# A causal-attention mixer on one core: the second halves of the first batch's probabilities go through TensorE, and the planner is told when to load w_ch1

## The chip, the cores and the metric

The kernel runs on one core of one Trainium2 chip. The metric is device time in microseconds (us); lower is better. A core has five engines that run side by side, each with its own in-order queue: TensorE (PE, whose weight loads the profile lists as PEld), VectorE (DVE), ScalarE (ACT), GpSimd (POOL) and SyncE (SP, whose queue here issues every DMA).

## The reference, cut to what matters

Three stages run one after the other on two batches of 448 tokens, twelve heads of width 64, 768 channels:

```python
scores = scale * q @ k.T                      # causal mask, per head: 448 x 448
attn = exp(scores - max) / sum                # 24 (batch, head) pairs
x = attn @ v                                  # -> (2, 448, 768)
u = x + (relu(x.T @ w_tok1) @ w_tok2).T       # token mixing, 448 -> 256 -> 448
y = u + relu(u @ w_ch1) @ w_ch2               # channel mixing, 768 -> 1536 -> 768
h = gelu(y @ w_in); a, b = split(h)           # 768 -> 1024
out = y + (a * (w_sg @ norm(b) + b_sg)) @ w_out
```

The weights arrive in 64-bit floats. Each operand of a product is split into a high and a low part, and a product is three matmuls (high x high, high x low, low x high).

## The kernel before

**Attention.** A head's 448 queries are four tiles (one of 64 rows, three of 128). They are worked in two halves of 512 key columns each: half 0 holds tiles 0 and 3, half 1 holds tiles 1 and 2 (`HALVES`). There are 2 batches x 12 heads x 2 halves = 48 halves; a step n of the main loop (`order`) is one head, so two halves. `pair` runs two heads that share a tile of PSUM for the values.

`probabilities` makes one half: TensorE computes the scores into PSUM (line 284); VectorE negates, scales, masks and reduces them to the negated maximum `mx` in one pass (L289), then adds the logarithm of PSCALE = 32768 to the two maxima in a small instruction of 128x2 (L294, `bias`); ScalarE takes the exponential (L296), so that `pe` holds probabilities times 32768; ScalarE casts them to 16 bits (L298, the high half of `hl`); GpSimd subtracts that from `pe` (L299, the low half); and one DMA on SP's queue transposes both halves at once into `pT` (L301). `values` (L324 to L326) multiplies `pT` by the values on TensorE.

**Values.** `prep_v` splits the values of a pair of heads into 16-bit parts with a scale (L253 to L261), and uses one PSUM slot of the pool `ps_e` (two slots) for a small matmul.

**Token mixing.** After every fourth head `token_mix` runs for that group: `a_ps`, then `u_ps` (L375, L377), which also adds x by fp32 transposes on TensorE (L384), then the split into `u_hi` and `u_lo` (L386, L387). The token weights are loaded at step n = 3 (`load_tok`).

**Channel mixing.** `channel_up(m, batches)` loads one tile of w_ch1 (`load64`: a DMA at L105 on SP into one of two `wraw` slots, ScalarE at L112, VectorE at L113 to L115, ScalarE at L119, GpSimd at L94), then does 18 matmuls (`r_ps`, L134 to L136) per batch. For m from 0 to 6 (`NF0` = 7) batch 0 is done in the attention part, with a PSUM slot of `ps_e`; in program order the first stands after step (1, 6) and the other six behind the loop. Everything after (`channel_up` for batch 1, `channel_down`, the gated part) is a dense run of matmuls.

**Order of the work.** The order on each engine is not the program's: a planner simulates a timeline when the kernel is built, and takes what is ready by priority, where program order is the priority (`prep_v` is moved ahead by 80). So a channel_up that stands late in the program is a filler: it goes where the planner's timeline has room. What the planner has laid down is then fixed on each in-order queue.

Of the kernel before, what the change touches and what calls it, by code (L numbers as in the profile page):

```python
# [10 lines left out]
F16 = mybir.dt.float16  # L11
F32 = mybir.dt.float32
F32R = mybir.dt.float32r
I32 = mybir.dt.int32
AF = mybir.ActivationFunctionType
ALU = mybir.AluOpType
# [3 lines left out]
PSCALE = 32768.0  # L20
# [7 lines left out]
def mixer_kernel(  # L28
# [18 lines left out]
    nc = tc.nc  # L47
    B, H2, D2, S = q.shape
    H, D = 2 * H2, D2 // 2
# [3 lines left out]
    P = 128  # L53
# [10 lines left out]
    def f32(ap):  # L64
        return ap.bitcast(F32)
# [5 lines left out]
    ident = const.tile([P, P], F32, name="ident")  # L71
# [21 lines left out]
    def sub(lo, src, hi):  # L93
        nc.gpsimd.tensor_sub(lo, src, f32(hi))  # L94
# [27 lines left out]
    def load_w(src):  # L122

        k = src.shape[1]
        hi = wpool.tile([P, WC // P, P], F32R, tag="whi", name="whi", bufs=3)[:, :k, :]
        lo = wpool.tile([P, WC // P, P], F32R, tag="wlo", name="wlo", bufs=3)[:, :k, :]
        load64(hi.rearrange("p a f -> p (a f)"), lo.rearrange("p a f -> p (a f)"), src.rearrange("p a f -> p (a f)"))
        return hi, lo

    def mm3(ps, pairs, begun=False):  # L130

        n = len(pairs)
        for i, ((lh, ll), (rh, rl)) in enumerate(pairs):
            nc.tensor.matmul(ps, lh, rh, start=i == 0 and not begun, stop=False)  # L134
            nc.tensor.matmul(ps, lh, rl, start=False, stop=False)  # L135
            nc.tensor.matmul(ps, ll, rh, start=False, stop=i == n - 1)  # L136
# [19 lines left out]
    NP = 512  # L156
# [8 lines left out]
    rpool = rs.enter_context(tc.tile_pool(name="rpool", bufs=1))  # L165
    r_of = {}

    def channel_up(m, batches, pool, psum):

        wh, wl = load_w(w_ch1[m])  # L170
        for b in batches:
            us = slice(b * S, (b + 1) * S)
            pr = psum.tile([P, 512], F32, tag="d", name="r_ps")
            mm3(pr[:, :S], [((wh[:, c, :], wl[:, c, :]), (u_hi[:, c, us], u_lo[:, c, us])) for c in range(NCC)])
            rh = pool.tile([P, S], F32R, tag=f"rh{m}_{b}", name="rh")
            rl = pool.tile([P, S], F32R, tag=f"rl{m}_{b}", name="rl")
            nc.scalar.activation(rh, pr[:, :S], AF.Relu)
            nc.vector.scalar_tensor_tensor(rl, pr[:, :S], 0.0, f32(rh), ALU.max, ALU.subtract)
            r_of[m, b] = (rh, rl)
# [14 lines left out]
    with ExitStack() as at:  # L194
# [3 lines left out]
        hlp = at.enter_context(tc.tile_pool(name="hlp", bufs=2))  # L198
        stp = at.enter_context(tc.tile_pool(name="stp", bufs=6))
# [5 lines left out]
        ps_e = at.enter_context(tc.tile_pool(name="ps_e", bufs=2, space=PSUM))  # L205
# [18 lines left out]
        for i in range(NVT):  # L224
            hi = fixed.tile([P, NVC, 2, D + 2], F16, name=f"vh{i}")
# [5 lines left out]
        def load_tok():  # L231
            for c in range(NQ):
                load64(w1h[:, c, :], w1l[:, c, :], w_tok1[tok(c), :], "pool", twice=c == 0)
            for c in range(NT):
                load64(w2h[:, c, :], w2l[:, c, :], w_tok2[c * P:(c + 1) * P, :], "pool")
# [27 lines left out]

        count = [0]

        def probabilities(qp, k2, hd, half):

            ps = ps_s.tile([P, NP], F32, tag="s", name="s_ps")  # L270
            if (hd, half) == (1, 0):
                pe, mx = pes[count[0] % len(pes)], mxs[count[0] % len(pes)]
            else:
                pe = xp.tile([P, NP], F32, tag="pe", name="pe", bufs=NPE)
                mx = stp.tile([P, 2], F32, tag="mx", name="mx")
            todo, o = [], 0
            for j, i in enumerate(HALVES[half]):
                w = KW[i]
                if i > 0 or hd == 0:
                    todo.append((j, i, slice(o, o + w)))  # L280
                    q0 = S - 64 if i == 0 else S + w - P if hd else w - P - 64
                    for ks in KEYS[i]:
                        m = ks.stop - ks.start
                        nc.tensor.matmul(ps[:, o:o + m], qp[:, q0:q0 + P], k2[:, ks], start=True, stop=True)  # L284
                        o += m
                else:
                    o += w
            for j, i, cs in todo:
                nc.vector.tensor_tensor_reduce(  # L289
                    out=pe[:, cs], in0=ps[:, cs], in1=mask0 if i == 0 else mask[:, MASKS[i]],  # L290
                    scale=-1.0 / math.sqrt(D), scalar=3.0e38, op0=ALU.add, op1=ALU.min, accum_out=mx[:, j:j + 1],
                )
            bias = stp.tile([P, 2], F32, tag="bias", name="bias")
            nc.vector.tensor_scalar(bias, mx, math.log(PSCALE), None, ALU.add)  # L294
            for j, i, cs in todo:
                nc.scalar.activation(pe[:, cs], pe[:, cs], AF.Exp, bias=bias[:, j:j + 1], scale=-1.0)  # L296
            hl = hlp.tile([P, 2, NP], F16, tag="hl", name="hl", bufs=4)
            nc.scalar.copy(hl[:, 0], pe)  # L298
            nc.gpsimd.tensor_sub(hl[:, 1], pe, hl[:, 0])  # L299
            pT = hlp.tile([P, 2, NP // P, P], F16, tag="pT", name="pT", bufs=4)  # L300
            nc.sync.dma_start_transpose(  # L301
                out=pT.rearrange("p a c q -> p (a c) q"), in_=hl.rearrange("p a n -> p (a n)")
            )
            return pT


# [21 lines left out]
        def pair(b, e, qk, vs, x):  # L328

            (vh, vl, sv), (xf, xh, xl) = vs, x  # L330
            px = ps_x.tile([P, 7, D + 1], F32, tag="x", name="x_ps")
            for hd in range(2):
                for half in range(2):
                    pT = probabilities(*qk, hd, half)
                    values(px, pT, hd, half, vh, vl)
                if hd == 0:
                    yield
            count[0] += 1
            rd = stp.tile([P, 7, 1], F32, tag="rd", name="rd")
            nc.vector.tensor_scalar(rd, px[:, :, D:D + 1], 1e-9 * PSCALE, sv[:, 0:1], ALU.add, ALU.mult)  # L340
            nc.vector.reciprocal(rd, rd)
            nc.vector.tensor_mul(xf[:, e], px[:, :, :D], rd.to_broadcast([P, 7, D]))
            cs = slice(e * P, (e + 1) * P)
            x6 = xf[:, e, 1:].rearrange("p (c h) d -> p c (h d)", h=2)
            nc.scalar.copy(xh[:, 1:, cs], x6)
            sub(xl[:, :, cs], x6, xh[:, 1:, cs])

            for h in range(2):
                hs, ls = (slice(64 * i, 64 * i + 64) for i in (h, 1 - h))
                ds = slice(e * P + h * D, e * P + h * D + D)  # L350
                nc.gpsimd.tensor_scalar(xh[hs, 0, ds], xf[hs, e, 0], 1.0, 0.0, ALU.mult, ALU.add)
                sub(xh[ls, 0, ds], xf[hs, e, 0], xh[hs, 0, ds])

        def token_mix(b, g, xf, xh, xl):
# [13 lines left out]
            for e in range(N // P):  # L368
# [17 lines left out]
                nc.scalar.copy(u_hi[:, cc, us], pu[:, :S])  # L386
                nc.vector.tensor_sub(u_lo[:, cc, us], pu[:, :S], f32(u_hi[:, cc, us]))  # L387

        order = [(b, h) for b in range(B) for h in range(H)]
        qks, vss = {}, {}  # L390

        def prepare(n):
            if n < len(order):
                b, h = order[n]
                if h % 2 == 0:
                    qks[b, h // 2] = prep_qk(b, h // 2)

        def prepare_v(n):
            if n < len(order) and n % 2 == 0:
                b, h = order[n]  # L400

                with tc.high_priority(offset=-80):
                    vss[b, h // 2] = prep_v(b, h // 2)

        dense = list(range(NF0))
        for n in range(AHEAD):
            prepare(n)
        for n in range(VAHEAD):
            prepare_v(n)
        for n, (b, h) in enumerate(order):  # L410
            prepare(n + AHEAD)
            prepare_v(n + VAHEAD)
            if n == GH - 1:
                load_tok()
            if h % GH == 0:
                x = (
                    xp.tile([P, GH // 2, 7, D], F32, tag="xf", name="xf", bufs=2),
                    xp.tile([P, NQ, GH * D], F32R, tag="xh", name="xh"),
                    xp.tile([P, NQ - 1, GH * D], F32R, tag="xl", name="xl"),
                )  # L420
            if h % 2 == 0:
                it = pair(b, h % GH // 2, qks[b, h // 2], vss[b, h // 2], x)
            next(it, None)
            if h % GH == GH - 1:
                token_mix(b, h // GH, *x)

            if (b, h) == (1, H // 2):
                channel_up(dense.pop(0), [0], rpool, ps_e)

        for m in dense:  # L430
            channel_up(m, [0], rpool, ps_e)


    NDC = 4
# [172 lines left out]
```

## Time and profile before

| | |
|---|---|
| time, median of 3 runs | 440.64 us (436.31, 440.64, 441.17) |
| the profiled execution's own time | 436.57 us |
| its span, first to last instruction | 434.8 us |
| PE busy | 403.1 us, 93% |
| DVE busy | 322.8 us, 74% |
| POOL busy | 251.4 us, 58% |
| ACT busy | 196.9 us, 45% |
| mean granted TensorE clock | 0.984 of full |

Busy times are unions over the whole span; TensorE's matmuls overlap one another and their ends are modelled, so a busy PE is not PE at its peak. The attention part fills about the first 165 us; the rest of the span is the dense run.

### The profile page before, as it was taken

To read this page: it belongs to the slowest core of one execution; us is meant where nothing else is said; L and a number is where in the kernel's file an instruction comes from. 1 tells how busy PE (TensorE), PEld (TensorE's weight loads), DVE (VectorE), ACT (ScalarE), POOL (GpSimd) and SP (SyncE) were. 2 spreads that over 40 slices of the span, in tenths; PEclk is the share of its full clock that TensorE was granted. 3 is DMA by queue.
4 is the path that set the end of the run, shared out by engine and by line. 5 is a ranking of instruction groups with operands and counts; after the bars stand their busy time and mean duration, and the time that the engine had idled before them with its cause. 6 is when DMAs were issued, how large, how long until landed. Compare 5 with 4: busy or idle time off the path is not lost. (4 is left out here: it accounts for less than half of the span.)

```text
span 434.8 us, 7061 instructions
## 1 busy us (share of the span) xinstructions
PE 403.1 (93%) x2567; PEld 340.1 (78%) x2567; DVE 322.8 (74%) x623; ACT 196.9 (45%) x341; POOL 251.4 (58%) x234
## 2 busy tenths in 40 slices
PE   5786897879879999999999999999999999999996
PEld 3363676667758899899999999999898889965995
DVE  5999996769999669889878677877786744159422
ACT  2777677575957544435344333333334133322200
POOL 2678877935996945456242355545539574225572
PEclk9999999969999999999999999999999999999999
DMA  7899999999798943534564533443434200200122
GB/s 206 179 211 235 221 182 216 196 247 239 181 190 218 168 147 95 197 145 146 148 190 131 157 100 121 123 144 121 154 133 139 93 0 6 92 2 1 64 107 84
DMA packets 66739, 62.30 MB, mean 143 GB/s; under 512 B 53136, under 2 KB 58384, under 8 KB 66704
## 3 DMA queue, kind: packets, MB, share of 16 engines
q1 hardware_dynamic: 66704, 61.85, 54.5%
q8 instruction: 20, 0.33, 0.3%
q14 instruction: 15, 0.12, 0.1%
HBM read 46.50 MB, written 2.75 MB: 113 GB/s over the span
## 5 line engine op out<-in xcount | busy, mean ns | idle before, releaser
L94 POOL TENSOR_TENSOR wlo<-wm,whi 128x768 fp32r<-128x768 f32 (+1 forms) x41 | 83.3, 2033 | 59.3 <-ACT whi L119 54.1
L112 ACT ACTIVATE wm<-wraw 128x768 f32<-128x768 f32 (+2 forms) x53 | 42.7, 808 | 79.1 <-DMA wraw<-in 39.6
L299 POOL TENSOR_TENSOR hl<-pe,hl 128x512 f16<-128x512 f32 x48 | 60.9, 1279 | 29.1 <-ACT hl L298 25.3
L284 PE MATMUL s_ps<-k,q 128*128 128x64 f32 (+3 forms) x216 | 58.9, 414 | 16.9 <-DVE mx L289 9.9
L113 DVE TENSOR_SCALAR wm<-wm 128x768 int32<-128x768 int32 (+2 forms) x53 | 34.2, 647 | 51.5 <-ACT wm L112 51.3
L114 DVE SCALAR_TENSOR_TENSOR wm<-wraw,wm 128x768 int32<-128x768 int32 (+2 forms) x53 | 64.7, 1221 | 0.8
L115 DVE SCALAR_TENSOR_TENSOR wm<-wraw,wm 128x768 int32<-128x768 int32 (+2 forms) x53 | 64.6, 1221 | 0.8
L296 ACT ACTIVATE pe<-pe,bias 128x192 f32<-128x192 f32 (+3 forms) x84 | 39.6, 523 | 33.0 <-DVE bias L294 32.6
L284 PEld LDWEIGHTS s_ps<-k,q 128*128 128x128 f32 x216 | 31.9, 207 | 28.9 <-DVE mx L289 11.5
L135 PE MATMUL r_ps<-u_lo,whi 128*128 128x448 f32 x144 | 53.4, 371 | 0.5 <-DVE u_lo L387 0.4
L134 PE MATMUL r_ps<-u_hi,whi 128*128 128x448 f32 x144 | 53.2, 370 | 0.0
L136 PE MATMUL y_ps<-rh,wlo 128*128 128x448 f32 x144 | 52.7, 366 | 0.3 <-POOL wlo L94 0.3
L136 PE MATMUL r_ps<-u_hi,wlo 128*128 128x448 f32 x144 | 52.7, 366 | 0.0
L134 PE MATMUL y_ps<-rh,whi 128*128 128x448 f32 x144 | 52.6, 366 | 0.0
L135 PE MATMUL y_ps<-rl,whi 128*128 128x448 f32 x144 | 52.6, 366 | 0.0
L119 ACT CAST whi<-wm 128x768 fp32r<-128x768 f32 (+1 forms) x41 | 32.7, 798 | 28.2 <-PE ug_ps L135 11.1
L289 DVE CUSTOM_DVE_ANT_0 pe<-s_ps,mask 128x192 f32<-128x192 f32 (+3 forms) x84 | 34.6, 439 | 4.4 <-PE s_ps L284 4.4
L94 POOL TENSOR_TENSOR u_lo<-yt,u_hi 128x448 fp32r<-128x448 f32 x12 | 15.3, 1273 | 35.5 <-ACT u_hi L191 35.5
L298 ACT CAST hl<-pe 128x512 f16<-128x512 f32 x48 | 28.6, 611 | 7.8 <-DMA pT<-hl 7.7
L324 PE MATMUL x_ps<-vh,pT 128*128 128x65 f16 (+1 forms) x240 | 26.3, 198 | 6.3 <-DMA pT<-hl 6.2
L324 PEld LDWEIGHTS <-pT 128*128 128x128 f16 (+1 forms) x240 | 21.4, 99 | 13.4 <-DMA pT<-hl 7.2
L135 PEld LDWEIGHTS r_ps<-u_lo,whi 128*128 128x128 f32 x144 | 27.2, 189 | 3.5 <-DVE u_lo L387 1.3
(141 smaller groups left out, 949.9 us busy)
## 6 DMA issues: line engine op xcount, KB each, us to landing
wraw<-in SPq DMA_DIRECT2D x35, 768.0 KB, 4.4
wraw<-in SPq DMA_DIRECT2D x14, 512.0 KB, 3.8
vr<-in SPq DMA_DIRECT2D x12, 320.0 KB, 3.5
k<-in SPq DMA_DIRECT2D x12, 224.0 KB, 3.4
q<-in SPq DMA_DIRECT2D x24, 112.0 KB, 3.6
out<-ob SPq DMA_DIRECT2D x12, 224.0 KB, 1.9
wraw<-in SPq DMA_DIRECT2D x3, 256.0 KB, 3.3
pT<-hl SPq DMA_TRANSPOSE x48, 3.5
```

Source lines behind the costliest of these rows:

```text
L94: nc.gpsimd.tensor_sub(lo, src, f32(hi))
L112: nc.scalar.activation(m, words.bitcast(F32)[:, :, 1], AF.Abs, scale=2.0 ** -112)
L114: nc.vector.scalar_tensor_tensor(mi, words[:, :, 1], -0x80000000, mi, ALU.bitwise_and, ALU.bitwise_or)
L115: nc.vector.scalar_tensor_tensor(mi, words[:, :, 0], 29, mi, ALU.logical_shift_right, ALU.bitwise_or)
L134: nc.tensor.matmul(ps, lh, rh, start=i == 0 and not begun, stop=False)
L135: nc.tensor.matmul(ps, lh, rl, start=False, stop=False)
L136: nc.tensor.matmul(ps, ll, rh, start=False, stop=i == n - 1)
L284: nc.tensor.matmul(ps[:, o:o + m], qp[:, q0:q0 + P], k2[:, ks], start=True, stop=True)
L289: nc.vector.tensor_tensor_reduce(out=pe[:, cs], in0=ps[:, cs], in1=mask0 if i == 0 else mask[:, MASKS[i]], scale=-1.0 / math.sqrt(D), scal ...
L296: nc.scalar.activation(pe[:, cs], pe[:, cs], AF.Exp, bias=bias[:, j:j + 1], scale=-1.0)
L299: nc.gpsimd.tensor_sub(hl[:, 1], pe, hl[:, 0])
L324: nc.tensor.matmul(o, ph, vh[:, c, h, :D + 1], start=j == 0, stop=False)
```

## The change

For batch 0 and half 1 (two per pair of heads, six pairs: 12 of the 48 halves) the probabilities are no longer cast, subtracted and transposed by DMA. The exponential takes `mx` itself as its bias, so `pe` is at most 1; TensorE transposes it in four fp32 pieces of 128x128 into a PSUM slot of `ps_e`; ScalarE writes the high half from PSUM with the factor 32768; VectorE writes the low half from PSUM in one pass. For the other 36 halves the sum with log(PSCALE) is taken by ScalarE (`nc.scalar.add`) and not by VectorE. The main loop records after each step the last DMA transpose that was issued, and every `channel_up` of the attention part puts its SP instructions (its w_ch1 load) behind the transpose of step 10 + m; the first of them moves in program order from behind step (1, 6) to behind step (1, 10).

```diff
-        def probabilities(qp, k2, hd, half):
+        def probabilities(qp, k2, hd, half, on_pe):
...
-            bias = stp.tile([P, 2], F32, tag="bias", name="bias")
-            nc.vector.tensor_scalar(bias, mx, math.log(PSCALE), None, ALU.add)
+            bias = mx
+            if not on_pe:
+                bias = stp.tile([P, 2], F32, tag="bias", name="bias")
+                nc.scalar.add(bias, mx, math.log(PSCALE))
             for j, i, cs in todo:
                 nc.scalar.activation(pe[:, cs], pe[:, cs], AF.Exp, bias=bias[:, j:j + 1], scale=-1.0)
+            pT = hlp.tile([P, 2, NP // P, P], F16, tag="pT", name="pT", bufs=4)
+            if on_pe:
+                tp = ps_e.tile([P, 512], F32, tag="d", name="t_ps")
+                for c in range(NP // P):
+                    cs = slice(c * P, (c + 1) * P)
+                    nc.tensor.matmul(tp[:, cs], pe[:, cs], ident, is_transpose=True, start=True, stop=True)
+                hi, lo = (pT[:, i].rearrange("p c q -> p (c q)") for i in range(2))
+                nc.scalar.activation(hi, tp, AF.Copy, scale=PSCALE)
+                nc.vector.scalar_tensor_tensor(lo, tp, PSCALE, hi, ALU.mult, ALU.subtract)
+                return pT
             hl = hlp.tile([P, 2, NP], F16, tag="hl", name="hl", bufs=4)
             nc.scalar.copy(hl[:, 0], pe)
             nc.gpsimd.tensor_sub(hl[:, 1], pe, hl[:, 0])
-            pT = hlp.tile([P, 2, NP // P, P], F16, tag="pT", name="pT", bufs=4)
-            nc.sync.dma_start_transpose(
+            last[0] = nc.sync.dma_start_transpose(
                 out=pT.rearrange("p a c q -> p (a c) q"), in_=hl.rearrange("p a n -> p (a n)")
-            )
+            ).ins
             return pT
...
-                    pT = probabilities(*qk, hd, half)
+                    pT = probabilities(*qk, hd, half, b == 0 and half == 1)
...
+        last, marks = [None], []
         order = [(b, h) for b in range(B) for h in range(H)]
...
         dense = list(range(NF0))
+
+        def up():
+
+            m = dense.pop(0)
+            with tc.issue_after(marks[H - 2 + m]):
+                channel_up(m, [0], rpool, ps_e)
...
             next(it, None)
+            marks.append(last[0])
             if h % GH == GH - 1:
                 token_mix(b, h // GH, *x)
 
-            if (b, h) == (1, H // 2):
-                channel_up(dense.pop(0), [0], rpool, ps_e)
-
-        for m in dense:
-            channel_up(m, [0], rpool, ps_e)
+            if (b, h) == (1, H - 2):
+                up()
+
+        while dense:
+            up()
```

## Rows read from the trace of the kernel before

**Rows 1.** Busy time per engine by stretch: us busy (instructions), clock, DMA share, GB/s.
```profile
...
0.00:87.00 87.00, 68.06 (x652) 47.77 (x652) 74.81 (x253) 56.25 (x113) 62.81 (x85) 0.98 0.94 206
87.00:165.00 78.00, 69.69 (x616) 59.02 (x616) 65.79 (x143) 49.41 (x89) 55.25 (x58) 0.93 0.84 194
165.00:435.00 270.00, 265.32 (x1302) 233.27 (x1300) 182.25 (x228) 91.24 (x140) 133.37 (x93) 1.00 0.34 108
...
```

**Rows 2.** The same, 10 to 60 us and stretches after it.
```profile
...
10.00:60.00 50.00, 40.26 (x379) 26.39 (x379) 49.08 (x152) 35.28 (x72) 38.02 (x42) 0.97 0.95 207
60.00:87.00 27.00, 22.98 (x264) 18.25 (x262) 20.82 (x79) 18.33 (x38) 22.69 (x30) 1.00 1.00 204
90.00:100.00 10.00, 10.00 (x82) 7.94 (x80) 8.35 (x17) 7.99 (x16) 4.97 (x4) 0.76 1.08 227
...
```

**Rows 3.** Waits, 0 to 87 us: us in total, times, longest.
```profile
...
ACT pe L296 <- DVE bias L294: 18.5, 10, 6.6
...
PEld s_ps L284 <- DVE mx L289: 8.9, 9, 2.0
PE s_ps L284 <- DVE mx L289: 7.8, 13, 1.3
...
```

**Rows 4.** Groups of instructions, VectorE, 10 to 60 us: busy us, mean ns.
```profile
...
L294 DVE TENSOR_SCALAR bias<-mx 128x2 f32<-128x2 f32 x22 | 9.5, 435 | 0.0
L261 DVE SCALAR_TENSOR_TENSOR vl<-vr,sv,vh 128x640 f16<-128x640 f32 x5 | 7.7, 1546 | 0.6 <-ACT vh L260 0.6
...
```

**Rows 5.** Timeline of VectorE, L294 twice: start us, us.
```profile
...
12.55 0.15 DVE L294 TENSOR_SCALAR bias<-mx 128x2 f32<-128x2 f32 x1
...
56.33 0.86 DVE L294 TENSOR_SCALAR bias<-mx 128x2 f32<-128x2 f32 x1
...
```

**Rows 6.** Groups by shape, 0 to 250 us: busy us, mean ns, idle before.
```profile
...
L299 POOL TENSOR_TENSOR hl<-pe,hl 128x512 f16<-128x512 f32 x48 | 60.9, 1279 | 29.1 <-ACT hl L298 25.3 <-DMA pT<-hl 3.1 <-DVE bias L294 0.3
...
L298 ACT CAST hl<-pe 128x512 f16<-128x512 f32 x48 | 28.6, 611 | 7.8 <-DMA pT<-hl 7.7
...
L294 DVE TENSOR_SCALAR bias<-mx 128x2 f32<-128x2 f32 x48 | 18.8, 402 | 0.1
...
L296 ACT ACTIVATE pe<-pe,bias 128x448 f32<-128x448 f32 x24 | 15.8, 658 | 2.7 <-DVE bias L294 2.7
...
L296 ACT ACTIVATE pe<-pe,bias 128x64 f32<-128x64 f32 x12 | 4.1, 346 | 19.5 <-DVE bias L294 19.5
L365 DVE SCALAR_TENSOR_TENSOR al<-a_ps,ah 128x512 fp32r<-128x512 f32 x6 | 4.1, 680 | 0.9 <-ACT ah L364 0.9
...
L364 ACT ACTIVATE ah<-a_ps 128x512 fp32r<-128x512 f32 x6 | 3.5, 589 | 0.4 <-PE a_ps L136 0.4
...
```

**Rows 7.** DMA queue totals (packets, MB, share) and transposes issued, 0 to 87 us.
```profile
...
q1 hardware_dynamic: 34663, 17.80, 93.6%
...
pT<-hl SPq DMA_TRANSPOSE x29, 3.6
...
```

**Rows 8.** DMA queue totals, 190 to 300 us.
```profile
...
q1 hardware_dynamic: 3164, 15.71, 46.3%
...
```

**Rows 9.** What touches pT, whole span: ns min/median/max, first and last start.
```profile
...
L301 SPq DMA_TRANSPOSE pT<-hl x48: 1232/1264/5275, 11.5 to 149.5; - x48
...
DMA to landing us min/median/max: 3.0/3.5/9.0
```

**Rows 10.** Timeline of TensorE: three fp32 transposes of 128x128.
```profile
...
60.19 0.52 PE L384 MATMUL u_ps<-ident,xf 128*128 128x128 f32 x3
...
```

**Rows 11.** Timeline of SP: the first w_ch1 load; four transposes.
```profile
...
79.69 0.58 SPq L105 DMA_DIRECT2D wraw<-in  x1
...
85.73 9.58 SPq L301 DMA_TRANSPOSE pT<-hl  x4
...
```

**Rows 12.** Waits, 87 to 165 us.
```profile
...
ACT pe L296 <- DVE bias L294: 14.1, 9, 5.0
...
```

**Rows 13.** Busy time of what touches r_ps, one stretch.
```profile
...
100.00:150.00 50.00, 12.74 (x54) 10.40 (x54) 1.85 (x3) 1.60 (x3) 0.97 0.91 199
...
```

## Prediction

> **What bounds the kernel now.** I read the stretches first: which engine is full where. From 165 us on TensorE is busy 265.3 of 270 us [rows 1]: the dense run has no room, and the change does not touch it, so it can only gain or lose ahead of 165 us. There TensorE is busy 68.1 us in 0 to 87 (19 idle) and 69.7 in 87 to 165 (8.3 idle) [rows 1]: about 27 us is the most that could come out. In 10 to 60 us VectorE is the full engine, 49.1 of 50, while TensorE has 40.3 [rows 2]. From 60 to 87 VectorE drops to 20.8 of 27 and the DMA engines show a share of 1.00 [rows 2]: there the transposes queue.
>
> The waits say the same. In 0 to 87 ScalarE's exponential waited 18.5 us for L294 on VectorE, and TensorE's score matmuls and their weight loads 7.8 and 8.9 us for VectorE's maxima, which free the PSUM of the scores [rows 3]. So batch 0 goes at VectorE's pace first and at the transposes' pace later; batch 1 is closer to TensorE's, because dense work fills it.
>
> What fills VectorE is partly not work. L294 handles two numbers per partition and takes 435 ns on average, 9.5 us in those 50 [rows 4]; alone it takes 0.15 us, and 0.86 in a bad place [rows 5]. POOL was running in 38 of the 50 us [rows 2], and L261 is stretched beside it, 1546 ns [rows 4].
>
> **The change, part by part.**
>
> *Maxima's term.* VectorE loses all 48 L294 (18.8 us, 402 ns each, [rows 6]): 24 x 0.42 = 10 us in batch 0, some 9 in batch 1. ScalarE gains 36 sums of 128x2. No such row exists. Above: the exponential over 64 columns, 346 ns; below: zero gain or loss, if it lies wholly in ScalarE's wait. I extrapolate the exponential's own rows: (658 - 346) / (448 - 64) = 0.81 ns a column [rows 6], so 0.30 us at 2 columns, 36 x 0.30 = 11 us. ScalarE has 56.3 us busy of 87 and 49.4 of 78 [rows 1], and it waited 18.5 us for exactly this term, so I cost it at zero on the path; if that cover is gone it costs at most 0.35 x 36 = 12 us on ScalarE's queue. Behind the sum stands only the exponential that needed it anyway.
>
> *Twelve halves by TensorE.* Removed per half: ScalarE's cast (611 ns), GpSimd's subtraction (1279 ns), one DMA transpose. Added: four transposes, an eviction on ScalarE and one on VectorE. ScalarE: a 128x512 eviction from PSUM took 589 ns against 611 [rows 6], zero. VectorE: L365, the same operation from PSUM on 128x512, took 680 ns [rows 6]: 12 x 0.68 = 8.2 us added, all in batch 0. GpSimd: 12 x 1.28 = 15 us less of its 62.8; the stretching of VectorE beside it should shrink with it. L261 at 1546 ns would save most; I take 2 us for the stretch, with 0 and 5 as ends.
>
> DMA: in 0 to 87 the queue moved 17.80 MB at a share of 93.6%, 81.4 us; 29 transposes of 0.262 MB are 7.6 MB of it [rows 7]. Loads alone, later, move 15.71 MB at 46.3% of 110 us [rows 8], 0.309 MB per us. So the loads of batch 0 are 10.2 / 0.309 = 33 us and a transpose is (81.4 - 33) / 29 = 1.67 us of all engines: twelve are 20 us, and the share falls from 0.94 to about 0.70. SP's queue loses 12 issues of 1.26 us, 15 us, and each half that goes over TensorE no longer has the median 3.5 us from issue to landing [rows 9]; q, k and v loads queued behind those issues go out earlier. The four `hl` slots turn over less, too.
>
> TensorE: three transposes of this kind took 0.52 us [rows 10], so 0.13 us for each more, about 0.65 us for four and 12 x 0.6 = 7 us in all. They lie in batch 0, where 19 us were idle [rows 1]: zero, as long as they are not waited for (rival 2). Their PSUM slot is one of `ps_e`'s two, shared with the small matmul of `prep_v`; it is held from transposes to VectorE's pass, about 2 us, six pairs: zero, with VectorE's queue as cover.
>
> *The w_ch1 pacing.* Each of seven loads may not pass the transpose of step 10 + m on SP. Before, the first left at 79.69 us [rows 11], behind the 27th transpose, which is step 13: already later than step 10. The edge holds back nothing that was so late; it only stops the planner from pulling loads into the freed batch 0, where their three VectorE passes would hurt. I cost it at zero; bounds: a gain of at most a load's VectorE time; the loss is rival 1's.
>
> *Sum.* Batch 0, VectorE: -10 + 8.2 - 2 = -4 us. Batch 0, the transpose-bound 60 to 87: VectorE had 6 us free there, four transposes held SP for 9.58 us at its end [rows 11], and with the DMA load down by a quarter I take -3 of it (0 to -6). Batch 1: VectorE loses 9 us, ScalarE's wait for L294 was 14.1 us [rows 12], but TensorE had only 8.3 us idle [rows 1]: I take -2 (0 to -6). Together **-9 us**, ends -2 and -19.
>
> The sum stands against the profiled run's 436.6 us (434.8 span and 1.8 around it): 427.6. That run was 4 us under the median of 440.6; from the median it would be 431.6. I say **430**.
>
> **Rivals.**
>
> 1. *It moves nothing (within 1%).* VectorE leaves the path but TensorE's fillers come later: the first channel_up now stands four steps later in program order. Before 150 us some 12.7 us of r_ps work was in the attention part [rows 13]. If two thirds of that move behind it, 8.5 us of the 9 are given back: 436 to 440. For it: TensorE's room ahead of 165 us is small. Against: the fillers were set by the planner's room, not by where they stand, and six of seven stood last already.
>
> 2. *TensorE waits in its queue for the exponential (slower).* The transposes sit in TensorE's in-order queue and need both exponentials of their half; scores and values of other halves stand behind them. Before, scores already waited there for VectorE 22 times for 16.7 us, 0.76 us each, up to 2.0 [rows 3]. Twelve groups at 0.76 us cost 9 us and cancel the gain: that is the point from which it decides. At 1.8 us (maximum passes plus two exponentials) it is 22 us, 13 more than gained: 450. Against: the planner can put values of an older half in between, and waits of this size fall into 19 us that were idle.
>
> 3. *More than forecast.* All far ends of the sum at once, 19 us: 418 to 422. It needs batch 1 to follow too.
>
> 4. *The clock.* In 90 to 100 us the granted clock was 0.76 [rows 2], after a stretch in which TensorE waited for transposes: part of that stretch was at 1.2 and not 2.4 GHz, and 2.4 us of 10 were lost. If the new transposes left TensorE at the lower level around them, six stretches like 90 to 100, one per pair, would be 14 us more TensorE time; with 7 us of transposes that overfills the 19 idle by 2, and no gain is left: 438 to 445. The Trainium skill, TensorE: Matmul & The Clock Gate, Part 4, states such a rule: the full clock does not engage for matmuls in transpose mode. The rows bear little of it out: the fp32 transposes at 60.19 us ran in a stretch at clock 1.00 [rows 2, 10], short and between other matmuls, as the new ones will.
>
> That the change does not do what it says is possible for the pacing alone (an edge that never binds), and is inside the forecast.
>
> **How the numbers follow.** Forecast 0.48, rival 1 0.27, rival 2 0.12, rival 3 0.08, rival 4 0.05. A measurement here can tell about 1% from no change; 1% under the median is 436.2. Faster: 0.48 + 0.08 = 0.56; same 0.27; slower 0.17. The forecast's own range is 422 to 437, some five us around its two levels 427.6 and 431.6. To reach 8 in 10 it takes in rival 1 and the mild end of rival 2: 421 to 442. Likeliest 430.
>
> **What would show it.** Right: VectorE no longer near 98% in 10 to 60 us; no wait of the exponential for VectorE of the size in [rows 3]; DMA share in batch 0 near 0.7; batch 0's token mixing for its last group done some 7 us earlier (before, r_ps work could begin after 110 us); TensorE's busy time in 0 to 87 up by the transposes. Wrong: TensorE's transposes with waits above 0.75 us each; r_ps work in the attention part well under 12.7 us before the last values; VectorE as full as before, because channel_up's passes moved into the room; granted clock in batch 0 well under 0.98.

## The result, and the profile after

The changed kernel took **442.67 us** (median of 20 runs, 438.94 to 448.5) against 438.58 (434.0 to 441.92) before, a ratio of **1.0105 [1.0073, 1.0138]**; a second set of its runs gave 1.0141 [1.0094, 1.0188], median 443.99. It is about 1% slower; 430, and a range up to 442, were forecast. The profile of the first set caught a disturbed, longer execution, so the rows below are of the second set (d_after_again): 438.5 us span, clock 0.980.

Its busy time by stretch, as in [rows 1, 2]:

```profile
0.00:87.00 87.00, 69.58 (x672) 51.94 (x673) 73.35 (x225) 59.10 (x127) 46.32 (x73) 0.94 0.77 186
87.00:165.00 78.00, 72.16 (x653) 61.08 (x652) 59.09 (x135) 51.65 (x112) 59.81 (x58) 0.98 0.75 182
165.00:438.00 273.00, 265.46 (x1294) 233.57 (x1292) 179.73 (x227) 90.84 (x140) 132.34 (x93) 0.99 0.33 106
...
10.00:60.00 50.00, 41.56 (x414) 30.59 (x413) 47.65 (x139) 37.17 (x83) 28.93 (x38) 0.97 0.77 172
```

What was to be removed was removed: GpSimd has 28.9 us in 10 to 60 where it had 38, and the DMA share in 0 to 87 fell from 0.94 to 0.77 (about 0.70 was forecast). But VectorE is at 47.65 of 50, against 49.1: almost as full as before. Three of VectorE's costliest lines there (line, operation, count, busy us and mean ns):

```profile
L289 DVE CUSTOM_DVE_ANT_0 pe<-s_ps,mask 128x448 f32<-128x448 f32 (+3 forms) x34 | 14.2, 439 | 0.5 <-PE s_ps L284 0.5
L261 DVE SCALAR_TENSOR_TENSOR vl<-vr,sv,vh 128x640 f16<-128x640 f32 x6 | 6.2, 1030 | 0.0
L307 DVE SCALAR_TENSOR_TENSOR pT<-t_ps,pT 128x512 f16<-128x512 f32 x8 | 5.5, 682 | 0.5 <-ACT pT L306 0.5
```

L294's 9.5 us [rows 4] are gone, eight of the new evictions L307 are in, and L261 is shorter beside a GpSimd that works less. Batch 0's last value matmul does come 6 us earlier, at 74.29 us against 80.24 before (L337 of the changed kernel is the old L326):

```profile
80.24 0.20 PE L326 MATMUL x_ps<-vh,pT 128*128 128x65 f16 x1
```

```profile
74.29 0.19 PE L337 MATMUL x_ps<-vh,pT 128*128 128x65 f16 x1
```

But the last division of batch 0 (its output `xf` closes the sixth pair) starts at 83.48 us, against 83.29 before:

```profile
83.29 0.62 DVE L342 TENSOR_TENSOR xf<-x_ps,rd 128x448 f32<-128x448 f32 x1
```

```profile
77.87 0.21 DVE L351 TENSOR_SCALAR rd<-x_ps,sv 128x7 f32<-128x7 f32 x1
...
79.07 2.46 DVE L114 SCALAR_TENSOR_TENSOR wm<-wraw,wm 128x768 int32<-128x768 int32 x1
...
82.62 0.94 DVE L115 SCALAR_TENSOR_TENSOR wm<-wraw,wm 128x768 int32<-128x768 int32 x1
83.48 0.61 DVE L353 TENSOR_TENSOR xf<-x_ps,rd 128x448 f32<-128x448 f32 x1
```

Ahead of it VectorE works the passes of two w_ch1 tiles, six of 128x768 with 6.7 us in all; before the change the first of them started at 87.9 us, behind that division. And by 87 us VectorE had done 53 of its 84 passes over scores (L289), where it had done 60: part of the 6 us is order alone, with batch 1's scores later.

And a new hole opened at the end of attention. TensorE, 165 to 180 us, the rows with an idle time in front, the last a_ps row and the r_ps rows on either side:

```profile
167.45 0.37 PE L136 MATMUL r_ps<-u_hi,wlo 128*128 128x448 f32 x1
...
169.80 0.28 PE L136 MATMUL a_ps<-xh,w1l 128*128 128x256 f32 x1
171.60 0.47 PE L386 MATMUL u_ps<-w2h,ah 128*128 128x448 f32 x1 [1.52 <-ACT ah L375]
...
174.64 0.47 PE L386 MATMUL u_ps<-w2h,al 128*128 128x448 f32 x1 [1.97 <-DVE al L376]
...
178.65 0.45 PE L134 MATMUL r_ps<-u_hi,whi 128*128 128x448 f32 x1
```

The r_ps matmuls up to 167.45 us are the last of the 126 that the seven channel_ups of batch 0 give as filler. From there to 178.65 nothing is left to fill with: TensorE waits for the last token mixing's evictions, 1.52 and 1.97 us, and its clock falls:

```profile
170.00:180.00 10.00, 6.51 (x28) 5.66 (x28) 8.06 (x10) 3.51 (x6) 2.47 (x1) 0.83 0.53 181
```

3.5 us of these 10 are idle, and 0.17 of the clock is lost. In the kernel before TensorE was busy 9.41 of 10 there, at clock 1.00:

```profile
170.00:180.00 10.00, 9.41 (x48) 7.82 (x47) 9.33 (x11) 4.43 (x7) 3.22 (x2) 1.00 0.50 176
```

How far the filler is used up can be read in one window: r_ps work from 60 us to the last of the values (x_ps, 158.4 us), 83 matmuls:

```profile
60.00:158.40 98.40, 18.89 (x83) 15.53 (x83) 2.48 (x4) 2.14 (x4) 0.95 0.79 194
```

Before, the same window (to 157.3 us) has 72: then 54 were left for the chain of the last pair and the last token mixing, now 43.

```profile
60.00:157.30 97.30, 16.60 (x72) 13.55 (x72) 1.85 (x3) 1.60 (x3) 0.95 0.92 203
```

And the chain itself is long. VectorE in the hole:

```profile
171.94 2.05 DVE L115 SCALAR_TENSOR_TENSOR wm<-wraw,wm 128x768 int32<-128x768 int32 x1
173.91 0.68 DVE L376 SCALAR_TENSOR_TENSOR al<-a_ps,ah 128x512 fp32r<-128x512 f32 x1
```

The `al` that TensorE waits for 1.97 us stands behind a pass of a w_ch1 load, 2.05 us; as long as there is filler, such a place in the queue costs nothing.

### The profile page after: what moved, and what is told of

It reads as the page before. It is cut to its first block, busy times and chain, and to the rows that moved or that the text cites. A ratio compares the mean times of both kernels' runs of the same rounds, so it can differ in the third digit from the quotient of the medians.

```text
span 446.7 us, 7098 instructions
## 1 busy us (share of the span) xinstructions
PE 411.4 (92%) x2615; PEld 349.9 (78%) x2615; DVE 314.2 (70%) x587; ACT 201.9 (45%) x377; POOL 236.7 (53%) x222
## 5 line engine op out<-in xcount | busy, mean ns | idle before, releaser
L94 POOL TENSOR_TENSOR wlo<-wm,whi 128x768 fp32r<-128x768 f32 (+1 forms) x41 | 80.8, 1973 | 70.1 <-ACT whi L119 60.8
L284 PE MATMUL s_ps<-k,q 128*128 128x64 f32 (+3 forms) x216 | 60.8, 425 | 10.6 <-DMA q<-in 4.9
L311 POOL TENSOR_TENSOR hl<-pe,hl 128x512 f16<-128x512 f32 x36 | 47.9, 1338 | 35.0 <-ACT hl L310 32.5
L115 DVE SCALAR_TENSOR_TENSOR wm<-wraw,wm 128x768 int32<-128x768 int32 (+2 forms) x53 | 63.5, 1198 | 0.8
L284 PEld LDWEIGHTS s_ps<-k,q 128*128 128x128 f32 x216 | 33.9, 219 | 22.2 <-issue 6.8
L289 DVE CUSTOM_DVE_ANT_0 pe<-s_ps,mask 128x192 f32<-128x192 f32 (+3 forms) x84 | 34.8, 442 | 5.5 <-PE s_ps L284 4.7
L335 PE MATMUL x_ps<-vh,pT 128*128 128x65 f16 (+1 forms) x240 | 27.2, 201 | 9.1 <-DVE xf L353 5.0
L136 PEld LDWEIGHTS y_ps<-rh,wlo 128*128 128x128 f32 x144 | 27.0, 188 | 3.8 <-POOL wlo L94 1.8
L298 ACT ACTIVATE pe<-pe,bias 128x448 f32<-128x448 f32 (+3 forms) x60 | 29.2, 533 | 0.5
```

The costliest lines, as they stand in the source:

```text
L115: nc.vector.scalar_tensor_tensor(mi, words[:, :, 0], 29, mi, ALU.logical_shift_right, ALU.bitwise_or)
L289: nc.vector.tensor_tensor_reduce(out=pe[:, cs], in0=ps[:, cs], in1=mask0 if i == 0 else mask[:, MASKS[i]], scale=-1.0 / math.sqrt(D), scal ...
L335: nc.tensor.matmul(o, ph, vh[:, c, h, :D + 1], start=j == 0, stop=False)
```

## Experiments

Diffs are against the kernel before where they say "before", else against the changed kernel. Ratios are to the kernel before as it was timed beside each set of runs, with 95% intervals; every profile is one execution.

**The parts alone.** First each part by itself, and the changed kernel again:

```diff
# a_bias_only, from before: all 48
-            nc.vector.tensor_scalar(bias, mx, math.log(PSCALE), None, ALU.add)
+            nc.scalar.add(bias, mx, math.log(PSCALE))
# b_pe_only, from before: the `if on_pe:` block of the change and nothing else
# c_pace_only, from before: marks, issue_after and the later first channel_up only
```

> The kernel before with the maxima's term on ScalarE for all 48 halves and nothing else of the change. Theory T (TensorE's added transposes and the clock around them cost the time): this keeps the gain on VectorE without the cost, 3 to 6 us faster than before. Theory P (the w_ch1 loads, now let out behind the 11th and 12th transposes, hold ScalarE's queue at the end of batch 0): also faster, 3 to 6 us. Theory B (ScalarE's small sums at the head of its queue hold what stands behind them): 2 to 5 us slower than before.

> The kernel before with only the twelve halves on TensorE; the other maxima's terms stay on VectorE, loads of w_ch1 free as before. Theory T: 3 to 6 us slower than before. Theory P: the loads are let out even earlier than in the change since SP is freer, so 4 us slower or more. Theory B: same as before or up to 4 us faster.

> The kernel before with only the loads of w_ch1 put behind the transposes and the first channel_up moved four steps later. Theory T and theory B: same as before within 1.5 us. Theory P: 2 to 5 us slower.

> The changed kernel once more, for its time beside the others and for a profile nearer its median: 4 us slower than before (ratio 1.007 to 1.014), with ScalarE's wait for the first w_ch1 load at the end of batch 0 there again, some 4 us.

Measured: the maxima's term **0.9844 [0.9809, 0.988]**, median 429.78, the lowest ratio of all kernels run; the halves 1.0183 [1.0144, 1.0221]; the pacing 1.0085 [1.0051, 1.0119]. So two of the three parts, each alone, cost time. With the term alone VectorE comes down:

```profile
10.00:60.00 50.00, 38.80 (x373) 26.44 (x372) 40.35 (x132) 36.62 (x92) 39.06 (x42) 0.95 1.07 209
```

40.35 us where the whole change has 47.65, with GpSimd as busy as before.

**Two of three.**

```diff
# e_bias_pace: no TensorE halves
-                    pT = probabilities(*qk, hd, half, b == 0 and half == 1)
+                    pT = probabilities(*qk, hd, half, False)
# f_pe_bias: no pacing
-            with tc.issue_after(marks[H - 2 + m]):
-                channel_up(m, [0], rpool, ps_e)
+            channel_up(m, [0], rpool, ps_e)
# g_pe_pace: the term on VectorE again
-                nc.scalar.add(bias, mx, math.log(PSCALE))
+                nc.vector.tensor_scalar(bias, mx, math.log(PSCALE), None, ALU.add)
```

> The change without the TensorE halves: maxima's term on ScalarE and the paced loads. Theory T (TensorE's transposes cost the time): 3 to 6 us faster than before. Theory P (paced loads hold ScalarE's queue): slower than the maxima's term alone by 2 to 5 us. Theory B (small sums on ScalarE): 2 to 5 us slower than before.

> The change without the pacing: TensorE halves and maxima's term on ScalarE, w_ch1 loads free. Theory P with the edge as the cost: 3 to 5 us faster than the change, so level with before. Theory T: as slow as the change, 4 us over before. If the edge is what keeps the loads from coming far too early, it is slower than the change.

> The change with the maxima's term back on VectorE for the 36 halves. Theory T: as slow as the change or 3 us slower still (VectorE loses its relief). Theory B: level with before. Theory P: as slow as the change.

Measured: 0.9849 [0.9804, 0.9893], 1.0122 [1.0081, 1.0162], 0.9966 [0.9934, 0.9998]. The halves cost 2.6 to 2.9% on top of the term (e to the whole change; a to f, 2.8%), but gain 1.2% on the pacing alone (c to g). Pacing changes nothing on top of the term (a to e) and of the other two (f to the whole). Effects that depend so much on company are no prices of instructions; something common moves. The filler is such a thing: r_ps matmuls ahead of the last values are 36 in e, 41 in g, 83 in the whole change, 108 in f. But the count alone does not order the kernels: a, the fastest, has 81.

**The transposes themselves, and the loads' time.**

```diff
# h_no_transpose: pT from pe, without transposing
-                tp = ps_e.tile([P, 512], F32, tag="d", name="t_ps")
-                ... four transposes
-                nc.scalar.activation(hi, tp, AF.Copy, scale=PSCALE)
+                nc.scalar.activation(hi, pe, AF.Copy, scale=PSCALE)
# (and L307 likewise)
# i_double: every transpose twice
+                    nc.tensor.matmul(tp[:, cs], pe[:, cs], ident, is_transpose=True, start=True, stop=True)
# j_late_pace: loads behind transposes four steps later
-            with tc.issue_after(marks[H - 2 + m]):
+            with tc.issue_after(marks[H + 2 + m]):
# k_half_pe: six halves, not twelve
-b == 0 and half == 1)
+b == 0 and half == 1 and hd == 0)
```

> The changed kernel with TensorE's 48 transposes and their PSUM slot left out: ScalarE and VectorE write pT straight from pe, so the values of these twelve halves are multiplied by probabilities that are not transposed. Theory T (TensorE's part up to 190 us has some 30 us of idle time that stays, so every microsecond of added TensorE work is paid): 5 to 8 us faster than the change, ratio to before 0.993 to 0.998. Theory V (the two evictions on ScalarE and VectorE and their place in those queues are the cost): as slow as the change, 1.01. Theory D (the DMA transposes gave something that is lost): 1.01 too.

> The changed kernel with every TensorE transpose issued twice (48 more instructions of the same kind, same result). Theory T: 5 to 7 us slower than the change, ratio to before 1.022 to 1.03. Theory V: within 1.5 us of the change. If transposes pull TensorE's clock down, more low-clock stretches and more than 7 us.

> The changed kernel with every w_ch1 load four steps later (behind the transpose of step 14 + m). Theory C (TensorE has used up its dense fillers before the last pairs of batch 1 are done, and stands idle at the lower clock near 170 to 180 us, 4 to 5 us): the stretch is filled and the time falls by 3 to 5 us, to 0.999 to 1.004 of before. Theory T alone: no change, 1.01.

> The change with half as many TensorE halves: only those of the first head of each pair, 6 of 48. Theory T: half the price of 11 us, so about 437, ratio to before 0.996 to 1.0. Theory C: between the two, either way by the planner's order. Theory V: half as well, so this tells T and V from a cost that comes with the first such half only (1.01).

Measured: 1.0101 [1.0061, 1.0141], 1.0019 [0.9987, 1.0052], 1.0105 [1.0062, 1.0149], 1.009 [1.0052, 1.0127]. Without the transposes it is no faster, with twice as many it is faster: their work on TensorE is not what makes the change slow. The order is again another: i has 52 r_ps matmuls ahead of the last values, h and k have 90 and 88. So i is better set beside l_hold3 below, which has no hole at the end of attention either: 1.0019 with 96 transposes, 1.0034 with 48. Later loads and half the halves give nothing back.

**The filler, moved on purpose.** `issue_after` puts an instruction behind another of the same queue; here the r_ps matmuls of the last channel_ups go behind the last values in TensorE's queue.

```diff
# l_hold3, l_hold5 (m >= 2); n_bias_hold3, n_bias_hold5: the same on a_bias_only
-            with tc.issue_after(marks[H - 2 + m]):
+            with ExitStack() as held:
+                held.enter_context(tc.issue_after(marks[H - 2 + m]))
+                if m >= 4:
+                    held.enter_context(tc.issue_after(lastv[0]))
# o_bias_early: a_bias_only, but all seven stand behind step (1, 0)
-            if (b, h) == (1, H // 2):
-                channel_up(dense.pop(0), [0], rpool, ps_e)
+            if (b, h) == (1, 0):
+                while dense:
+                    up()
```

> The changed kernel with the matmuls of the last five of the seven batch-0 channel_ups held in TensorE's queue behind the last values: 36 filler matmuls planned ahead of those, not 83. Theory C (fillers ahead of the last pairs delay them, and none is left for the wait after them): 4 to 8 us faster than the change, ratio to before 0.990 to 1.001, and the gap between the seventh and the eighth eviction of r_ps falls from 12.6 us to under 6. Theory X (the TensorE halves cost by something else): as slow as the change, 1.008 to 1.014.

> As the last, with three held (72 ahead of the last values, as before the change had 71). Theory C: part of the way, 1.000 to 1.008. Theory X: 1.008 to 1.014.

> The maxima's term alone (no TensorE halves, no pacing), with the last five batch-0 channel_ups held in TensorE's queue behind the last values (36 ahead, not 81). Theory C: 0.978 to 0.986 of before, level with or a little under the maxima's term alone (0.984). Theory X: no change from that.

> The maxima's term alone, with all seven batch-0 channel_ups standing behind step (1, 0) in program order, so that all 126 filler matmuls are planned ahead of the last scores. Theory C: the gain is lost, 8 to 16 us slower than the maxima's term alone, ratio to before 1.003 to 1.02, with a gap of 12 us or more ahead of the eighth eviction. Theory X: within 3 us of the maxima's term alone.

> The maxima's term on ScalarE alone with the last three fillers held behind the last values (72 of 126 ahead, not 81). Theory C: a little faster than the maxima's term alone, 0.978 to 0.984; if 81 was early enough, the same 0.984; with five held it was 1.0135, so a loss by starving TensorE would show as over 0.99.

Measured: holding three, **1.0034 [0.9997, 1.0071]**, five 1.0325 [1.0244, 1.0406]; on the term alone, three 0.991 [0.9867, 0.9953], five 1.0135 [1.0071, 1.0199]; all seven early 1.0504 [1.0442, 1.0567]. So the order alone, with not one instruction of the engines more or less, moves this kernel by 6.6% (a to o). On the term alone the hold of three did not help: a gain or no change was expected, and 0.9844 became 0.991. On the whole change it did. With three held, 72 r_ps matmuls stand ahead of the last values, about as many as before the change, and the hole at the end is closed:

```profile
170.00:180.00 10.00, 10.00 (x55) 9.18 (x54) 8.51 (x10) 5.00 (x8) 4.10 (x2) 1.00 0.53 162
```

That gives back 0.7 to 1.1%, three to five of the 438 us; the row of the whole change lost 3.5 us idle and 0.17 of the clock. In o_bias_early the same hole is wide, because all 126 were gone before the last values, at 184.6 us:

```profile
150.00:190.00 40.00, 22.18 (x285) 19.77 (x284) 20.11 (x43) 13.17 (x24) 19.23 (x26) 0.62 0.71 155
```

`al` stands behind a 2.08-us L115 in l_hold3 too, but TensorE has work meanwhile. With five held it is the other way round: 36 stand ahead, the hole at 170 to 180 is closed (busy 10.00), but TensorE stands idle ahead of it, and the filler that it did not use there is paid for later: from the last u_lo (180.14 us) to the end of the span it takes 270 us, against 259 in the whole change (179.50 to 438.5):

```profile
150.00:190.00 40.00, 33.95 (x221) 31.64 (x217) 19.20 (x31) 14.91 (x25) 14.45 (x16) 0.91 0.26 77
```

How many r_ps matmuls are left between the last a_ps and the u_ps that waits for its evictions tells the kernels apart better than how many stand ahead of the last values. TensorE's rows before the change:

```profile
167.40 0.28 PE L136 MATMUL a_ps<-xh,w1l 128*128 128x256 f32 x1
...
170.96 0.37 PE L136 MATMUL r_ps<-u_hi,wlo 128*128 128x448 f32 x1
171.16 0.37 PE L375 MATMUL u_ps<-w2h,ah 128*128 128x448 f32 x1
```

Eighteen r_ps matmuls lie between, and no wait. In the whole change the same eighteen went in among the a_ps matmuls (163.95 to 167.45 us) and none is left behind them. Counted in every trace: none in the whole change, b, f, h, j, k and o, which stand at 1.009 to 1.0504; 18 in l_hold3, n_bias_hold3, p and s, 23 in c, e, g and i, 7 in a, which stand at 0.9844 to 1.0085. Only the two kernels with five held (20 and 23) are slow with filler there; they had idled earlier. One trace each shows this, and only the hold of three moved it on purpose.

The Trainium skill, TensorE: Matmul & The Clock Gate, Part 2, "Step-by-step", says that matmuls stay in program order and only weight loads are pulled ahead; these runs agree, a filler that stands in the wrong place in the queue was not moved by the chip (0.9844 against 1.0504).

**What the halves still cost.** With three held, the halves cost 1.2% (0.991 to 1.0034; the first without the pacing, which changed nothing on top of the term). Two runs without the transposes take that apart: p leaves them out as h does, s moves the second pass to GpSimd besides.

```diff
# p_notp_hold3: l_hold3 with the edit of h_no_transpose
# s_pool_lo: p_notp_hold3 and
-                nc.vector.scalar_tensor_tensor(lo, pe, PSCALE, hi, ALU.mult, ALU.subtract)
+                nc.gpsimd.tensor_sub(lo, pe, hi)
```

> The changed kernel with the last three fillers held in TensorE's queue behind the last values, as l_hold3, and TensorE's 48 transposes left out (pT written straight from pe, so these halves are not transposed). 72 filler matmuls stand ahead of the last values in both. Theory T2 (with the fillers in place TensorE's 6 us of transposes are paid): 4 to 7 us faster than l_hold3, ratio to before 0.988 to 0.995. Theory V2 (the cost is in ScalarE's and VectorE's evictions or in the order of batch 0 and 1): 1.000 to 1.007, as l_hold3.

> The kernel p_notp_hold3 with one edit more: the second passes of the twelve halves (the rest of the probabilities) go to GpSimd as a subtraction of 128x512 and no longer to VectorE. It still leaves the transposition of these twelve halves out, and its rest lacks a scale; the operation has the same size. p_notp_hold3 stood at 1.006 to the kernel before, the sum on ScalarE with three held channel_ups and without the halves at 0.991. Theory 'VectorE's twelve passes of 0.68 us are what the halves still cost': VectorE loses 8.2 us in batch 0 and the ratio comes to 0.99 (0.985 to 0.995). Rival 'it is the order of the plan or the missing DMA transposes' place, not VectorE's load': it stays at 1.002 to 1.010. Second rival 'GpSimd's passes stretch VectorE's as before': between the two, about 0.997, with VectorE's first split of the probabilities (L261) longer again.

Measured: 1.006 [1.0019, 1.0101] and **0.9867 [0.981, 0.9923]**. Moving twelve passes of VectorE to GpSimd gave, by these ratios, 1.9% of 439, 8.5 us; twelve at 0.68 to 0.75 us are 8.2 to 9.0. The two were timed beside different runs of the kernel before, s with only four runs, and their own medians, 438.85 and 434.63, are 4.2 us apart: that the passes cost time is shown, the size lies between 4 and 8.5 us. VectorE in 10 to 60 us, p first (the two profiled executions, with spans of 435.4 and 434.6, hardly differ):

```profile
10.00:60.00 50.00, 39.93 (x398) 28.27 (x399) 45.77 (x142) 37.67 (x85) 29.91 (x36) 0.93 0.78 179
```

```profile
10.00:60.00 50.00, 39.92 (x357) 27.30 (x357) 41.28 (x131) 36.02 (x81) 39.87 (x42) 0.86 0.80 175
```

With the passes on GpSimd, L261 is stretched again (median 1156 ns in 0 to 87 us, against 876 in p), and the kernel is still faster. The Trainium skill, Perfetto Trace Analysis, "Optimizing Scalar/DVE Operations", warns that moving work between GpSimd and VectorE might not help because they share a port; here the stretch is there and the move pays all the same (1.006 to 0.9867).

## Why the prediction was wrong

The runs can be set in a row: the term alone with three held 0.991; the halves with their second pass on GpSimd 0.9867; that pass on VectorE 1.006; with the transposes 1.0034; without the hold, the whole change, 1.0105 and 1.0141. Only two steps are larger than their intervals: VectorE's passes, +1.9%, and the filler, +0.7 to 1.1%.

*Maxima's term.* The direction was right, and that ScalarE hides it: its sum took 199 ns on average, where 0.30 us was taken. The size was not: -10 in batch 0 and -2 in batch 1 were forecast, -7 us came (0.9844). Nor did it come where it was expected: in a_bias_only's trace batch 0's last division starts at 84.19 us, no earlier than before (83.29), and the last values are at 151.4 us, against 157.3. Why batch 0's end shows nothing of it is open.

*The evictions.* 12 x 0.68 us was the right price (L307 took 682 ns on average), and it lay on the path: all of it by the ratios of p and s, half of it by their medians.

*GpSimd's and DMA's relief (-2 and -3): the step that failed first.* The sum took relief in batch 0 for time of the kernel. Both resources were relieved, and batch 0's values ended 6 us earlier, but the kernel did not. In the whole change the passes of two early w_ch1 tiles stood ahead of the last division. In j_late_pace no such pass does, that division starts 5.7 us earlier than before, and the ratio is still 1.0105:

```profile
77.61 0.62 DVE L353 TENSOR_TENSOR xf<-x_ps,rd 128x448 f32<-128x448 f32 x1
```

So the relief did bring batch 0's end forward where no w_ch1 pass stood in its way, but batch 0's end did not set the kernel's. s_pool_lo says the same: it has the twelve DMA transposes less and none of the passes on VectorE, and its 0.9867 is no clear gain over the 0.9844 to 0.991 of the kernels with the term and without the halves. There GpSimd has its 39.87 us back, too, and the kernel is faster than p.

*The filler: the step that is missing from the sum.* Rival 1 looked at the right place with the wrong sign. It had the fillers come too late; they came too early and ran out before the last token mixing's evictions. The text's own sign for it (r_ps work before 150 us well under 12.7 us) did not show: that window has 54 matmuls in both kernels. What moved lies behind it: 83 ahead of the last values against 72, and none instead of 18 behind the last a_ps. The planner puts the queue together from its costs, and an edit in batch 0 changes its choice in batch 1; that was taken to be zero. It is 3 to 5 us here (l_hold3).

Together: -7 for the term, up to +8.2 for the passes, +3 to 5 for the hole give at most +4 to +6 us; 4.1 and 6.6 were measured. With 4 us for the passes the sum would be 0 to 2, so some 4 us of it rest on the ratios of p and s. Why the planner's choice falls as it does with each combination (c to g gains 1.2%, e to the whole loses 2.6) is not settled by these runs, and effects that do not add up leave the size of each term uncertain by some microseconds.

*The pacing.* "The edge holds back nothing that was so late" was wrong. In the changed kernel the halves free SP's queue, and the loads leave right behind transposes of batch 0. SP:

```profile
60.91 1.44 SPq L312 DMA_TRANSPOSE pT<-hl  x1
...
64.28 0.58 SPq L105 DMA_DIRECT2D wraw<-in  x1
65.87 1.26 SPq L312 DMA_TRANSPOSE pT<-hl  x1
67.18 0.87 SPq L105 DMA_DIRECT2D wraw<-in  x1
```

The first leaves at 64.28 us, against 79.69 before [rows 11]. Without the edge they would leave earlier still: in f_pe_bias eighteen passes of 128x768 stand on VectorE ahead of batch 0's last division, here six. So the edge binds, but step 10 is too early to keep those passes out of batch 0, which the prediction wanted of it. ScalarE stands 2.38 us at the head of its queue until the first load lands (d_after_again was expected to show some 4):

```profile
69.42 0.89 ACT L112 ACTIVATE wm<-wraw 128x768 f32<-128x768 f32 x1 [2.38 <-DMA wraw<-in]
```

j_late_pace, with the first load at 91.5 us, was no faster as a whole, so neither this wait nor those passes are what makes the change slow.

*Rival 2* (TensorE waits for the exponential) is refuted. The transposes and what they waited for:

```profile
L304 PE MATMUL t_ps<-ident,pe x48: 271/273/304, 14.5 to 69.4; 128*128 128x128 f32 x48
...
its engine sat idle before it (us, times) until:
  ACT pe L298: 1.3, 2
```

1.3 us in two waits, not 9 in twelve. *Rival 4* (clock) is refuted by i_double, with 96 transposes. All operations on t_ps by stretch (the first pair of numbers is TensorE's), two of five stretches with sixteen transposes:

```profile
30.00:40.00 10.00, 1.94 (x16) 1.73 (x16) 2.03 (x3) 1.17 (x2) 1.00 0.94 224
...
60.00:70.00 10.00, 2.08 (x16) 1.79 (x16) 1.02 (x2) 0.83 (x2) 1.00 0.53 131
```

All five have a granted clock of 1.00; the one stretch below it, 0.83 in 40 to 50 us, has eight, and it is 0.83 in the changed kernel with four as well. The Trainium skill, TensorE: Matmul & The Clock Gate, Part 4, states that the full clock does not engage in transpose mode: no run here has a stretch of transposes alone, and in these five, among other matmuls, the granted clock was full, 1.00.

## What to carry to other kernels

Relief in one stretch is not time of the whole kernel: here batch 0's values ended 6 us earlier, and nothing of it was left at the end, while twelve passes put on the fullest engine cost 4 to 8 us. Where a planner orders an in-order queue, count before and after an edit the filler that is left behind the last step of a dependent chain and ahead of the matmuls that wait for its evictions: none instead of 18 was worth 3 to 5 us here, and order alone moved this kernel by up to 6.6%. Time the parts of a change apart: one of three here, alone, is 1.6% faster than before, and beats the whole by 2.6%.

## What the runs showed that was not expected

Doubling the 48 fp32 transposes, 0.11 us apart, cost no time that shows (1.0019, against 1.0034 for l_hold3 with 48; neither has the hole). A ScalarE sum of 128x2 took 199 ns, half of VectorE's average of 402 ns for as many numbers [rows 6]. The clock fell to 0.83 over 10 us after two waits of 1.52 and 1.97 us.
